# A layer of S4 convolution and gated linear unit: one shuffle for the row exchange, joint table levels, whole casts, and a last stage by channel half

## The chip, the cores and the metric

The kernel runs on one core of a Trainium2 chip. A core has engines that run their own instruction queues side by side and meet through semaphores: TensorE (PE, matrix products, with PEld for its weight loads), VectorE (DVE), ScalarE (ACT), GpSimd (POOL) and SyncE (SP), which issues most DMAs. Operands lie in SBUF (128 partitions); PE writes to PSUM, from where DVE or ACT copy ("evacuate") to SBUF. The metric is the device time of one execution in microseconds, the median of several runs.

## The reference

With x = A_u of shape (1, 2048, 512) and layernorm xn of x over the 512 channels, the output is x + A(xn) + B(xn).

```python
def _A_ref(u, A_re, A_im, B_re, B_im, C_re, C_im, log_dt, Dskip):
    dt = jnp.exp(log_dt)[:, None]
    logdA, dB = dt * A, dt * Bc            # A, Bc, Cc complex, (512, 128)
    P = jnp.exp(logdA[:, :, None] * l[None, None, :])     # l = 0..2047
    K = jnp.einsum("dn,dnl,dn->dl", Cc, P, dB).real
    ...                                     # y = causal convolution of u with K along the tokens (by FFT)
    return y + u * Dskip[None, None, :]

def _B_ref(x, w_gate, w_up, w_down):        # 512 -> 1792 -> 512
    h = _sigmoid(x @ w_gate) * (x @ w_up)
    return h @ w_down
```

So branch A is a long convolution of each channel with a kernel made of 128 complex modes, and branch B is a gated linear unit.

## The kernel before

The program is a list of about 940 operations (`pl.add`, `pl.copy`), each with its engine, its dependences and the buffer slots that it takes and frees. A table written out by hand, `ORDER` (L207 on), gives the order in which `run` (L293 on) emits them, and so the order of every engine's queue. `ON_DVE` (L205) names by operation number the copies that go to DVE (L288) rather than ACT (L290); `UEV` (L204) names the up products that ACT evacuates (L1066), so that DVE multiplies them from SBUF (L1070).

In order of time, but heavily interleaved:

1. Warm-up products (L526), loads, and the layernorm of 16 tiles of 128 tokens: statistics L547 and L548, normalizing on ACT (L555) or DVE (L560). Tokens 0 to 511 are transposed by PE and evacuated by ACT (L576); the other three groups of four tiles go through DRAM (`x_scr`) and a transposing DMA.
2. Parameters of the modes (L613 and around), then a ladder of twelve powers (k = 0 to 11) of each mode's step: square on ACT (L672), the next power on DVE (L679, L681), and a cast of each power to bf16 into the tables `W` (L664 on DVE, L666 on ACT), two instructions a power, one for each channel half.
3. The first stage of the token transform (L698), stored to `z_scr` in DRAM.
4. The kernel tables, by four channel quarters (c = 0 to 3): from a seed copy, levels of complex products double a table `G` (1, 2, 4, 8 columns a level) and others a table `H`. Each product is four DVE instructions: multiplies L737 and L738, then sums L742 and L743, half as wide. Products of the tables on PE (L821), evacuation (L290), selection (L841) give the kernel's transform `kT`.
5. For each channel half (p = 0, 1; 256 channels) eight units: load from `z_scr`, product with the constant `m2` (L892), evacuation to `xx`, exchange of neighbouring groups of 32 partitions into the second row of `xx` (p = 0: four DMAs of 64 KB from SBUF to SBUF; p = 1: four DVE copies, L905), load of the constant `E` (320 KB), product with `kT` (L914), evacuation, elementwise products on DVE (L919, L923), product with the constant `mab` (L936), evacuation, and a store to `v_scr` in DRAM. The constants `m2` and `mab` are loaded once and serve both halves.
6. The gated unit, by four groups of 512 tokens: gate (L1031), up (L1055), sigmoid (L1043), product (L1070), down (L1099), fourteen products a tile. GpSimd's DMA adds x into the result (`glu_sb` for the first two groups).
7. The last stage, `final` (L999 on), for t = 0 to 5, two token tiles each: four products 512 wide (L995), one DVE sum (L1010) of the result and the down product's tile into a buffer of the pool `ot`, and an output DMA of 256 KB with runs of 2 KB. The last group of tokens is added by L1119.

The pools have few slots: two pairs of PSUM banks (pool `s`) are shared by stages 3 to 5 and 7, four single banks (pool `gu`) belong to the gated unit, three buffers each hold `xx` and `E`. PE runs its queue strictly in order, so that a product that waits holds up all that follow.

Of the kernel before, what the change touches and what calls it, by code (L numbers as in the profile page):

```python
# [12 lines left out]
I32 = mybir.dt.int32  # L13
# [7 lines left out]
D = 512  # L21
# [15 lines left out]
NU = 16  # L37
# [143 lines left out]
def _consts():  # L181
# [17 lines left out]
    for q in range(8):  # L199
        sr[q, q // 2, 31 + 32 * ((q ^ (q // 2)) % 2)] = 1.0  # L200
    return dict(SR=f(sr), ident=f(np.eye(128)), S1=f(np.tile(S1, (4, 1))), S2=f(np.stack([_build_S2(by), np.roll(_build_S2(by), 32, axis=1)], axis=1)), M2=f(quads(M2[by])), SW=f(sw),
                MAB=f(np.stack([quads(MA[by], True), quads(MB[by], True)], axis=2)), E=f(_build_E(M2, by).reshape(128, NU // 2, 2, NKT, 128).transpose(1, 0, 2, 3, 4)))

UEV = (3, 5, 8, 9, 10, 11, 15, 16, 17, 18, 19, 20, 21, 23, 24, 26, 27, 28, 29, 30, 31, 32, 33, 34, 35, 36, 37, 38, 39, 40, 41, 42, 43, 44, 45, 54)  # L204
ON_DVE = (64, 67, 73, 76, 97, 98, 110, 121, 122, 123, 124, 482, 836, 838)  # L205
ON_ACT = (2,)
ORDER = [  # L207
    1, 24, 0, 23, 2, 34, 25, 27, 4, 3, 6, 26, 33, 35, 37, 28, 36, 29, 30, 38, 43, 44, 46, 39, 40, 45, 10, 7, 13, 19,
    20, 31, 32, 21, 41, 48, 42, 22, 592, 604, 593, 605, 615, 618, 624, 47, 90, 88, 91, 49, 11, 103, 5, 14, 104, 89,
    606, 50, 102, 92, 93, 12, 627, 653, 658, 9, 633, 54, 594, 654, 55, 634, 610, 655, 101, 656, 106, 598, 611, 659,  # L210
    635, 599, 105, 616, 617, 619, 51, 94, 636, 56, 600, 95, 96, 97, 107, 657, 52, 628, 620, 621, 637, 15, 114, 622,
    643, 644, 57, 178, 108, 8, 98, 115, 645, 58, 625, 623, 110, 116, 53, 59, 640, 648, 142, 641, 601, 602, 626, 646,
    595, 596, 649, 143, 60, 117, 186, 631, 647, 612, 61, 613, 650, 629, 119, 109, 62, 63, 630, 597, 603, 614, 632, 65,
    99, 145, 638, 177, 118, 607, 660, 651, 100, 16, 661, 639, 180, 215, 168, 608, 652, 64, 66, 187, 609, 662, 642, 67,
    68, 169, 147, 704, 150, 726, 699, 148, 727, 179, 181, 190, 170, 151, 663, 149, 69, 127, 70, 188, 120, 664, 71, 121,
    171, 700, 665, 671, 72, 73, 172, 74, 189, 111, 130, 131, 146, 666, 75, 76, 122, 128, 216, 191, 77, 124, 192, 711,
    672, 705, 194, 195, 123, 125, 157, 158, 78, 159, 673, 709, 193, 719, 712, 79, 80, 196, 710, 160, 720, 739, 217,
    721, 740, 722, 724, 674, 679, 152, 197, 81, 82, 725, 680, 198, 173, 83, 723, 199, 713, 729, 684, 730, 686, 734,
    736, 737, 183, 112, 113, 685, 126, 84, 687, 200, 174, 86, 728, 201, 688, 735, 153, 154, 202, 689, 746, 690, 744,
    747, 745, 731, 667, 161, 738, 748, 203, 175, 85, 732, 204, 733, 129, 696, 184, 155, 205, 176, 716, 694, 697, 695,  # L220
    691, 692, 132, 714, 87, 715, 698, 206, 218, 207, 219, 717, 182, 706, 681, 775, 701, 693, 718, 135, 18, 185, 133,
    208, 210, 702, 707, 211, 682, 683, 136, 703, 220, 741, 144, 225, 233, 708, 742, 134, 156, 227, 209, 817, 812, 234,
    235, 162, 743, 237, 221, 813, 805, 230, 165, 238, 236, 749, 224, 806, 163, 241, 222, 242, 228, 226, 243, 223, 137,
    164, 17, 166, 244, 138, 139, 140, 141, 375, 239, 232, 229, 262, 675, 167, 750, 751, 752, 245, 246, 212, 757, 759,
    231, 758, 818, 213, 249, 810, 247, 240, 248, 250, 263, 251, 252, 214, 253, 811, 450, 376, 451, 377, 760, 452, 264,
    815, 800, 254, 255, 257, 265, 816, 814, 776, 275, 795, 272, 796, 258, 435, 378, 379, 381, 359, 777, 457, 274, 256,
    266, 819, 797, 765, 267, 280, 268, 281, 282, 309, 269, 283, 284, 259, 798, 801, 260, 261, 285, 454, 436, 820, 270,
    825, 273, 821, 360, 455, 382, 380, 456, 288, 277, 766, 453, 778, 826, 780, 781, 289, 799, 458, 459, 767, 785, 290,
    779, 442, 768, 437, 782, 383, 783, 278, 460, 291, 827, 802, 384, 438, 465, 367, 441, 439, 271, 461, 462, 361, 292,
    786, 769, 784, 286, 385, 293, 362, 828, 829, 463, 822, 790, 443, 823, 444, 276, 287, 386, 803, 279, 420, 440, 294,  # L230
    824, 310, 792, 851, 852, 466, 472, 390, 365, 445, 311, 364, 464, 296, 793, 467, 387, 412, 388, 791, 787, 832, 446,
    295, 298, 297, 794, 312, 299, 368, 830, 807, 369, 313, 788, 391, 392, 789, 447, 808, 448, 770, 473, 804, 300, 809,
    301, 363, 471, 366, 468, 405, 772, 370, 314, 474, 831, 771, 773, 302, 304, 319, 303, 305, 853, 856, 427, 394, 371,
    327, 833, 469, 470, 475, 397, 393, 395, 389, 449, 406, 421, 328, 774, 476, 407, 320, 329, 321, 422, 834, 331, 913,
    863, 398, 413, 914, 323, 854, 315, 332, 835, 396, 408, 330, 322, 496, 564, 426, 335, 399, 414, 316, 372, 477, 336,
    324, 837, 855, 337, 373, 374, 317, 338, 400, 326, 478, 857, 339, 340, 401, 318, 306, 428, 307, 429, 341, 308, 520,
    492, 342, 325, 343, 411, 425, 479, 568, 843, 493, 402, 345, 864, 403, 753, 761, 494, 333, 346, 344, 334, 423, 347,
    348, 424, 410, 430, 540, 845, 431, 349, 351, 838, 350, 352, 432, 565, 836, 433, 901, 404, 409, 906, 902, 415, 416,
    495, 353, 516, 528, 552, 566, 541, 354, 844, 881, 355, 569, 908, 567, 542, 882, 417, 570, 907, 434, 517, 903, 418,
    909, 518, 543, 556, 921, 419, 521, 497, 522, 571, 572, 861, 573, 498, 519, 523, 529, 846, 574, 910, 530, 883, 886,  # L240
    904, 524, 480, 504, 544, 905, 499, 508, 553, 862, 575, 525, 884, 554, 526, 885, 555, 865, 858, 557, 558, 545, 500,
    859, 839, 546, 866, 527, 484, 358, 847, 501, 502, 559, 560, 481, 911, 482, 561, 485, 868, 912, 562, 887, 589, 586,
    563, 547, 486, 915, 548, 483, 487, 505, 503, 532, 580, 356, 916, 509, 917, 506, 871, 510, 549, 869, 550, 551, 488,
    489, 872, 490, 491, 357, 891, 888, 583, 533, 896, 867, 873, 892, 507, 511, 531, 512, 893, 587, 874, 534, 513, 535,
    536, 537, 897, 514, 889, 894, 515, 898, 895, 875, 576, 918, 890, 870, 876, 899, 919, 878, 538, 539, 590, 588, 582,
    581, 577, 860, 578, 877, 591, 585, 579, 920, 900, 879, 880, 922, 840, 848, 925, 841, 842, 584, 849, 923, 926, 676,
    668, 850, 677, 669, 678, 670, 924, 927, 929, 762, 763, 930, 933, 754, 928, 764, 755, 756, 935, 934, 936, 931, 932,
    937, 939, 940, 938]
# [72 lines left out]
def kernel(  # L321
# [21 lines left out]
    pl = _Plan(dict(s=NS, gu=NGU, hT=NHT, zs=4, zx=2, xx=3, es=3, kb=2, pp=2, pq=2, vs=2, ot=3, tg=2, us=2, sq=2))  # L343
# [53 lines left out]
    for nm, sz in [("W1", 12 * KB), ("gc", 2 * KB), ("G", 16 * KB), ("H", 20992), ("tmp", 4 * KB), ("W0", 12 * KB),  # L397
                   ("xn", 16 * KB), ("lad", 16 * KB), ("kx", 8 * KB), ("zs", 4 * KB), ("pq", 2 * KB)]:
        OFF[nm] = o
        o += sz  # L400
# [5 lines left out]
    W = [at(OFF["W%d" % p], [12, 2, DW]) for p in range(NP)]  # L406
# [67 lines left out]
    l_m2 = load("SP", m2[:], cten["M2"].ap(), 256 * KB, pkt=2048)  # L474
# [186 lines left out]
    def f_cast(cur, k, dve):  # L661
        for p in range(NP):
            if dve:
                V.tensor_copy(out=W[p][:, k], in_=cur[:, :, DW * p:DW * p + DW])  # L664
            else:
                S.activation(out=W[p][:, k], in_=cur[:, :, DW * p:DW * p + DW], func=ACT.Identity)  # L666
# [59 lines left out]
    def cmul(lo, outp, n, m, conj, buf, deps, prio):  # L726

        ne = n * NPR * 4
        wide = lambda v: v.rearrange("p r c k h -> p r c (k h)")
        mre = m[:, 0, :].rearrange("p (r h) -> p r h", h=2).unsqueeze(2).to_broadcast([128, NPR, 2 * n, 2])  # L730
        mim = m[:, 1, :].rearrange("p (r h) -> p r h", h=2).unsqueeze(2).to_broadcast([128, NPR, 2 * n, 2])
        sl = _Slot(buf)
        tb = lambda: at(TMP[buf][sl.idx], [2048])[:, 0:ne].rearrange(
            "p (r c k h) -> p r c k h", r=NPR, c=2, h=2)
# [14 lines left out]
    for c in range(4):  # L749
# [5 lines left out]
        gdep = kgen.get(c - 2, [])  # L755
        hdep = kgen.get(c - 1, [])

        last = pl.copy(nc, 0.32, G[:, :, :, 0, :].rearrange("p r c h -> p c r h"),
                       gc[:, :, cs].rearrange("p c (r h) -> p c r h", h=2), [o_g] + gdep, PC)
        n = 1  # L760
        for lev in range(4):
            st = min(n, 8)
            for q in range(0, n, st):
                last = cmul(G[:, :, :, q:q + st, :], G[:, :, :, n + q:n + q + st, :], st, W[c // 2][:, 4 + lev, :, ws],
                            True, "tg", [last, W_op[4 + lev]], PC)
            n *= 2
# [428 lines left out]
```

## Time and profile before

| | us |
|---|---|
| median of three runs (222.06 to 223.08) | 222.13 |
| span of the profiled execution | 219.8 |
| PE, PEld busy | 209.2, 105.0 |
| DVE busy | 202.2 |
| ACT busy | 175.9 |
| POOL busy | 22.6 |
| evacuations and copies on ACT, L290 from 128x1024 PSUM, 63 of 1044 ns | 64.6 |
| sigmoids, L1043, 52 of 643 ns | 32.1 |
| products, L1070, from SBUF 36 of 421 ns; with a PSUM operand 20 of 684 ns | 14.9; 13.2 |
| exchange copies, L905, 32 of 421 ns, from 160.5 to 191.1 | 13.5 |
| DMA traffic | 41.36 MB, 188 GB/s mean |

The profile is one execution. Its span runs from the first to the last recorded instruction; the time of a run holds in addition what lies around it, here 2.3 us. A group's mean is the time of one instruction with what overlaps its neighbours. TensorE's granted clock is 1.00 in nearly every window. The slowest parts are not one after the other: PE, DVE and ACT are all busy most of the time, so what matters is which of them the others wait for in each stretch.

### The profile page before, as it was taken

What the parts mean: (1) busy time and instruction counts of PE and PEld (TensorE: products, weight loads), DVE (VectorE), ACT (ScalarE), POOL (GpSimd) and SP (SyncE); (2) the same over time, 40 slices, a digit from 0 to 9 for tenths busy, and PEclk for the clock granted to TensorE, in tenths of its full rate; (3) what the DMA queues carried; (4) which work ended last, traced back from release to release, by engine and by line L of the source; (5) the groups of instructions that cost most, each with busy time, mean ns of one, the idle gap of its engine ahead of it and who ended that gap; (6) DMA issues with size and microseconds to landing.
All of it is one profiled execution on the core that took longest, in us unless ns stands there. A gap on an engine that the chain in (4) does not pass through costs nothing.

```text
span 219.8 us, 5357 instructions
## 1 busy us (share of the span) xinstructions
PE 209.2 (95%) x2075; PEld 105.0 (48%) x2103; DVE 202.2 (92%) x444; ACT 175.9 (80%) x283; POOL 22.6 (10%) x39
## 2 busy tenths in 40 slices
PE   7999988999999999999999999999989999999994
PEld 2544433444434454445555555554555455543453
DVE  3999999999999999999999999999989999993582
ACT  3699999999999999769899999977578978942000
POOL 2216001001000049100000004000020100000000
PEclk9999999999999999999999999999999999999999
DMA  5997069216667064526818579856857987688743
GB/s 172 333 425 298 7 180 317 80 42 143 237 134 206 18 198 97 202 82 178 244 55 237 152 244 210 212 173 169 228 111 236 265 265 232 189 234 209 220 158 136
DMA packets 40651, 41.36 MB, mean 188 GB/s; under 512 B 9009, under 2 KB 31922, under 8 KB 40498
## 3 DMA queue, kind: packets, MB, share of 16 engines
q1 hardware_dynamic: 39458, 39.12, 57.7%
q0 software_dynamic: 864, 1.57, 4.9%
q10 hardware_dynamic: 304, 0.33, 0.6%
q8 instruction: 16, 0.26, 0.5%
q14 instruction: 9, 0.07, 0.1%
HBM read 25.28 MB, written 12.06 MB: 170 GB/s over the span
## 4 chain that ended last, share of the span: by engine, by line
DVE 48%; PE 41%; DMA 4%; ACT 4%; issue 2%; POOL 0%; DVEq 0%; ACTq 0%
PE bank L1099 11%; DVE big L738 7%; PE pair L914 7%; DVE big L737 6%; PE bank L1031 6%; PE bank L1055 6%; DVE hT_sb L1070 6%; PE pair L936 5%; DVE stats L547 4%; DVE big L742 4%; DVE big L743 3%; DVE big L679 3%; DVE big L681 3%; DMA big<-c_E 3%; ACT big L290 3%; DVE big L613 2%
## 5 line engine op out<-in xcount | busy, mean ns | idle before, releaser
L290 ACT ACTIVATE big<-pair 128x1024 bf16<-128x1024 f32 (+2 forms) x75 | 73.4, 996 | 9.2 <-PE pair L936 1.9
L1055 PE MATMUL bank<-xnT,wu_sb 128*128 128x512 bf16 x214 | 54.4, 379 | 2.5 <-ACT us_sb L1066 1.3
L1031 PE MATMUL bank<-xnT,wg_sb 128*128 128x512 bf16 (+1 forms) x211 | 50.9, 367 | 1.4 <-ACT xnT L576 0.4
L1099 PE MATMUL bank<-wd_sb,hT_sb 128*128 128x512 bf16 (+1 forms) x230 | 50.2, 366 | 0.4
L1043 ACT ACTIVATE hT_sb<-bank 128x512 bf16<-128x512 f32 x52 | 32.1, 643 | 3.8 <-PE bank L1031 3.6
L1031 PEld LDWEIGHTS <-wg_sb 128*128 128x128 bf16 x236 | 21.9, 98 | 26.4 <-issue 5.2
L1099 PEld LDWEIGHTS <-hT_sb 128*128 128x128 bf16 x238 | 22.5, 98 | 24.8 <-issue 2.1
L1055 PEld LDWEIGHTS <-wu_sb 128*128 128x128 bf16 x224 | 21.0, 97 | 27.2 <-issue 5.4
L737 DVE TENSOR_TENSOR big<-big 128x1024 bf16<-128x1024 bf16 (+4 forms) x40 | 26.8, 670 | 0.1
L738 DVE TENSOR_TENSOR big<-big 128x1024 bf16<-128x1024 bf16 (+4 forms) x40 | 26.6, 666 | 0.0
L1066 ACT ACTIVATE us_sb<-bank 128x512 bf16<-128x512 f32 x36 | 22.4, 634 | 0.0
L919 DVE TENSOR_TENSOR big<-big 128x2048 bf16<-128x2048 bf16 x16 | 19.5, 1219 | 0.4
L914 PE MATMUL pair<-big 128*128 128x256 bf16 x160 | 19.8, 272 | 0.1
L914 PEld LDWEIGHTS <-big 128*128 128x128 bf16 x160 | 15.5, 98 | 4.9 <-issue 1.1
L790 ACT ACTIVATE sq_sb<-big 128x256 bf16<-128x256 bf16 (+2 forms) x20 | 13.7, 685 | 3.9 <-DVE big L743 3.8
L743 DVE TENSOR_TENSOR big<-big 128x512 bf16<-128x512 bf16 (+4 forms) x40 | 16.6, 414 | 0.0
L742 DVE TENSOR_TENSOR big<-big 128x512 bf16<-128x512 bf16 (+4 forms) x40 | 16.5, 413 | 0.0
L290 ACT ACTIVATE big<-big 128x256 bf16<-128x256 bf16 x36 | 15.7, 470 | 0.2
L1070 DVE TENSOR_TENSOR hT_sb<-hT_sb,us_sb 128x512 bf16<-128x512 bf16 x36 | 14.9, 421 | 0.0
L905 DVE COPY big<-big 32x1024 bf16<-32x1024 bf16 x32 | 13.5, 421 | 0.5
L1070 DVE TENSOR_TENSOR hT_sb<-hT_sb,bank 128x512 bf16<-128x512 bf16 x20 | 13.2, 684 | 0.5 <-PE bank L1055 0.5
L936 PE MATMUL pair<-big 64*64 64x512 bf16 (+1 forms) x256 | 12.8, 326 | 0.5 <-ACT big L290 0.2
(103 smaller groups left out, 222.2 us busy)
## 6 DMA issues: line engine op xcount, KB each, us to landing
big<-c_E SPq DMA_DIRECT2D x16, 320.0 KB, 4.4
z_scr<-big SPq DMA_DIRECT2D x16, 256.0 KB, 3.0
big<-z_scr SPq DMA_DIRECT2D x16, 256.0 KB, 3.5
v_scr<-big SPq DMA_DIRECT2D x16, 256.0 KB, 2.9
big<-in_A_u_dram SPq DMA_DIRECT2D x4, 512.0 KB, 8.5
big<-big SPq DMA_DIRECT2D x32, 64.0 KB, 3.1
big<-v_scr SPq DMA_DIRECT2D x4, 512.0 KB, 5.0
wu_sb<-in_B_w_up_dram SPq DMA_DIRECT2D x2, 896.0 KB
```

What stands on the lines that cost most here:

```text
L290: nc.scalar.activation(out=get(out), in_=get(in_), func=ACT.Identity)
L737: V.tensor_tensor(out=wide(outp), in0=wide(lo), in1=mre, op=ALU.mult)
L738: V.tensor_tensor(out=wide(tb()), in0=wide(lo), in1=mim, op=ALU.mult)
L742: V.tensor_tensor(out=outp[:, :, 0], in0=outp[:, :, 0], in1=tb()[:, :, 1], op=opr)
L743: V.tensor_tensor(out=outp[:, :, 1], in0=outp[:, :, 1], in1=tb()[:, :, 0], op=opi)
L914: T.matmul(two(sk)[:, o:o + DW], es()[:, g, kt, :], kT[p][:, kt, :], start=kt in (0, NKT - 1), stop=kt >= NKT - 2)
L936: T.matmul(two(sv)[o:o + 64, DW * (2 * g + y):2 * DW * (g + 1)], mab[b:b + 64, 2 * u + g, q, :], pq()[b:b + 64, q, ch] if y else pp()[b:b ...
L1031: T.matmul(bank(sl, k % 2)[:, c0:c1], w_at(w, CUT_G, kt, k), xnT[:, grp, kt, c0:c1], start=(kt == 0), stop=(kt == KT - 1))
L1043: S.activation(out=hT_sb[:, hs.idx, k % 2, :], in_=bank(sl), func=ACT.Sigmoid)
L1055: T.matmul(bank(sl), w_at(wu_sb, CUT_U, kt, k), xnT[:, grp, kt, :], start=(kt == 0), stop=(kt == KT - 1))
L1070: V.tensor_tensor(out=h(), in0=h(), in1=us_sb[:, us.idx, :] if on else bank(sl), op=ALU.mult)
L1099: T.matmul(bank(po)[:, 0:c[1] - c[0]], hT_sb[:, hts[k // 2].idx, k % 2, jj * 128:(jj + 1) * 128], wd_sb[:, k, c[0]:c[1]], start=first and ...
```

## The change

The same result is computed. Six things differ.

- **Exchange of the second half (p = 1).** The four copies a unit become one `stream_shuffle` of 128 partitions by 512 int32 elements, which swaps neighbouring partitions within each group of 32. The rows of the constants are laid out to match, so `M2`, `MAB` and `E` now exist once for each half; `m2` (256 KB) is loaded again after the last L892 of the first half, `mab` (512 KB) after the last L936 of the first half.
- **Joint low levels.** For an even quarter c the seed and the levels of 1, 2 and 4 columns are made for quarters c and c+1 in one go (256 channels); the level of 8 stays with its quarter.
- **Whole casts.** A power is cast by one instruction of 1024 columns for both channel halves; `W0` and `W1` lie side by side for it.
- **Last stage.** `final` goes by group of four token tiles and channel half: eight products 256 wide, one DVE sum straight into the result's buffer, one output DMA of 256 KB with runs of 512 bytes. The first channel half's finals need only the first half's loads.
- **Engines.** 24 rather than 14 copies and normalizings are named in `ON_DVE` (with all normalizing from tile 4 on), 39 rather than 36 in `UEV`. Casts of the powers 0, 3 and 8 are on DVE, before those of 3, 4, 6 and 7.
- **Order.** `ORDER` is another list throughout. At the start, all warm-up products come ahead of the transposes; the first gate products are of full width, before four were of half the width.

```diff
+    pair = np.arange(32).reshape(2, 16)
+    alt = np.concatenate([(32 * np.array([[0], [1]]) + 2 * (pair % 16) + c).reshape(32) for c in range(2)])
+    alt = np.concatenate([alt, 64 + alt])
...
+    m2b[..., alt[0:64]], mabb[alt], eb[..., alt] = m2, mab, e
+    return dict(..., M2=f(np.stack([m2, m2b])), SW=f(sw),
+                MAB=f(np.stack([mab, mabb])), E=f(np.stack([e, eb])))
...
     def f_cast(cur, k, dve):
-        for p in range(NP):
-            if dve:
-                V.tensor_copy(out=W[p][:, k], in_=cur[:, :, DW * p:DW * p + DW])
-            else:
-                S.activation(out=W[p][:, k], in_=cur[:, :, DW * p:DW * p + DW], func=ACT.Identity)
+        src = cur.rearrange("p c (w d) -> p w c d", w=NP)
+        if dve:
+            V.tensor_copy(out=W_all[:, :, k], in_=src)
+        else:
+            S.activation(out=W_all[:, :, k], in_=src, func=ACT.Identity)
...
-        for lev in range(4):
-            st = min(n, 8)
-            for q in range(0, n, st):
-                last = cmul(G[:, :, :, q:q + st, :], G[:, :, :, n + q:n + q + st, :], st, W[c // 2][:, 4 + lev, :, ws],
-                            True, "tg", [last, W_op[4 + lev]], PC)
-            n *= 2
+        if c % 2 == 0:
+            G2 = at(OFF["G"], [2 * NPR, 2, NGE, 2])
+            last = pl.copy(nc, 0.48, G2[:, :, :, 0, :].rearrange("p r c h -> p c r h"),
+                           gc[:, :, DW * (c // 2):DW * (c // 2) + DW].rearrange("p c (r h) -> p c r h", h=2),
+                           [o_g] + kgen.get(c - 2, []) + hdep, PC)
+            for lev in range(3):
+                n = 1 << lev
+                last = cmul(G2[:, :, :, 0:n, :], G2[:, :, :, n:2 * n, :], n, W[c // 2][:, 4 + lev], True, "tg",
+                            [last, W_op[4 + lev]], PC)
+            g_part = last
+        g_done = cmul(G[:, :, :, 0:8, :], G[:, :, :, 8:16, :], 8, W[c // 2][:, 7, :, ws], True, "tg", [g_part, W_op[7]], PC)
...
+        if p:
+            l_m2 = dma("SP", m2[:], cten["M2"].ap()[1], deps=fm_op, prio=45, pkt=2048)(256 * KB)
+            l_mab = dma("SP", mab, cten["MAB"].ap()[1], deps=fv_op, prio=46, pkt=4096)(512 * KB)
...
                 def f_sw(xx=xx):
-                    for b in range(4):
-                        V.tensor_copy(out=half_of(xx, b, 1), in_=half_of(xx, b ^ 1, 0))
+                    q = lambda j: xx()[:, j].rearrange("p h m -> p (h m)").bitcast(I32)
+                    V.stream_shuffle(out=q(1), in_=q(0), mask=[i ^ 1 for i in range(32)])
...
-    def final(t, gdeps):
-        sl, osl = _Slot("s"), _Slot("ot")
+    def final(g, p, gdeps):
+        sl, cs = _Slot("s"), slice(DW * p, DW * p + DW)
+        res = (glu_sb[:, 4 * g:4 * g + 4, :] if g < 2 else at(TAIL["glu"], [4, D]))[:, :, cs]
...
-            for r in range(2):
-                s2_mm(t, r, bank(sl, r), True, (0, D))
+            for q in range(4):
+                for j in range(2):
+                    T.matmul(two(sl)[64 * j:64 * j + 64, DW * q:DW * q + DW], s2[:, q % 2, :], vall[:, g, p, j, q, :], start=True,
+                             stop=True, tile_position=(0, 64 * j), skip_group_check=True)
...
-            V.tensor_tensor(out=ot().rearrange("p r d -> p (r d)"), in0=two(sl), in1=res.rearrange("p r d -> p (r d)"), op=ALU.add)
+            V.tensor_tensor(out=res, in0=two(sl).rearrange("p (q d) -> p q d", q=4), in1=res, op=ALU.add)
...
-        dma("SP", outv[:, isl, :], lambda: ot(), deps=[fin], prio=1, rel=[osl], pkt=2048)(256 * KB)
+        dma("SP", outv[:, 4 * g:4 * g + 4, cs], lambda: res, deps=[fin], prio=1, pkt=512)(256 * KB)
```

## The prediction

> **What bounds the kernel now.** I read first the engines' totals, then the windows along the span, then the chain of waits, then the groups of instructions and the DMA issues.
>
> ```profile
> PE 209.2 (95%) x2075; PEld 105.0 (48%) x2103; DVE 202.2 (92%) x444; ACT 175.9 (80%) x283; POOL 22.6 (10%) x39
> ```
> ```profile
> core 0: us, PE busy (x) PEld busy (x) DVE busy (x) ACT busy (x) POOL busy (x), PEclk, DMA share, GB/s
> ...
> 30.00:50.00 20.00, 18.71 (x96) 8.02 (x98) 19.93 (x51) 19.80 (x35) 1.26 (x2) 1.00 0.47 145
> 50.00:70.00 20.00, 19.66 (x101) 8.46 (x102) 20.00 (x46) 20.00 (x35) 1.07 (x1) 1.00 0.67 176
> ...
> 130.00:150.00 20.00, 19.67 (x315) 11.22 (x319) 20.00 (x40) 17.47 (x29) 2.22 (x4) 1.00 0.78 206
> ...
> 160.00:180.00 20.00, 19.11 (x233) 10.94 (x234) 18.81 (x35) 17.37 (x22) 1.54 (x3) 1.00 0.81 218
> 180.00:200.00 20.00, 19.70 (x177) 10.30 (x180) 18.48 (x36) 13.59 (x19) 0.00 (x0) 1.00 0.78 224
> 200.00:219.80 19.80, 16.35 (x106) 8.43 (x104) 9.69 (x11) 0.59 (x1) 0.00 (x0) 0.99 0.57 176
> ```
> PE is busy 209.2 of 219.8 us, so 10.6 us are all that any order could win. Of these 1.4 lie ahead of the first matmul and 3.5 behind the last (add, store, landing). Some 5.7 us lie inside. From 30 to 150 us DVE is full, and PE is not: PE waits there for a full DVE. From 160 us both have gaps. The chain says the same:
>
> ```profile
> 84.63 1.13 DVE big L737
> 85.76 1.14 DVE big L738
> 87.54 1.09 DVE big L737
> ```
> ```profile
> 155.94 1.42 PE L821 MATMUL pair<-big 128*32 128x82 bf16 x128
> ...
> 161.63 0.44 PE L841 MATMUL pair<-big,sw 128*32 128x96 bf16 x24 [0.62 <-issue]
> ```
> The first fence has pieces of the chain (start, time on the chain), the second PE's timeline at the fourth quarter's tables (start, time, work, idle before). The chain runs from start to start of DVE's instructions, so it shows the price of one in a full queue, the step: an L737 of 1024 columns has a mean of 686 ns in the groups but a step of 0.60. I use steps where instructions follow each other, since each overlaps the next by some 0.08 us.
>
> ```profile
> L905 DVE COPY big<-big 32x1024 bf16<-32x1024 bf16 x32 | 13.5, 421 | 0.5
> L737 DVE TENSOR_TENSOR big<-big 128x1024 bf16<-128x1024 bf16 x16 | 11.0, 686 | 0.0
> L681 DVE TENSOR_TENSOR big<-big 128x512 f32<-128x512 f32 x11 | 7.6, 691 | 0.0
> L1010 DVE TENSOR_TENSOR big<-pair,glu_sb 128x1024 bf16<-128x1024 f32 x4 | 4.7, 1220 | 3.2 <-PE pair L995 3.2
> L664 DVE CAST big<-big 128x512 bf16<-128x512 f32 x8 | 3.1, 427 | 0.0
> ```
> ```profile
> big<-c_E SPq DMA_DIRECT2D x16, 320.0 KB, 4.4
> ...
> v_scr<-big SPq DMA_DIRECT2D x16, 256.0 KB, 2.9
> ...
> big<-c_MAB SPq DMA_DIRECT2D x1, 512.0 KB, 4.4
> ```
>
> **How far PE is behind.** I added the steps of PE's groups in its own order and compared with its real starts. PE is 0.6 us late at the first full gate matmul (12.7 us), 3.5 at the first down product (41.5), 4.8 at L821 of the fourth quarter (155.94 against 151.2 of work), 5.5 behind the L841 wait, 6.65 at the last down product (213.3). Most of the loss is therefore made by 156 us, where DVE's results are the gate.
>
> **The change on DVE.** Exchange: 32 copies of 0.42 (13.5 us) become 8 shuffles. No row shows a shuffle. Below it lies the 0.42 of a copy with the same columns on a quarter of the partitions; above it the 1.68 of the four copies that it replaces. I take 0.60, the step of L681, the nearest in columns and width (512 of 4 bytes): 4.8 us, so -8.7.
>
> The Trainium skill ("VectorE: DVE Perf Modes", section "The perf-mode tier table") speaks against it: a copy of bf16 in SBUF has a 4x mode, STREAM_SHUFFLE only the 1x mode, some 2400 ns for 2048 elements. Its formula for 1x, (N+151)/0.96, gives an estimate of 691 ns for 512 elements, which the trace's L681 agrees with; charged by 1024 bf16 elements it would be 1224, and the exchange would win 3.7 rather than 8.7.
>
> Joint levels: for each pair of quarters, 24 instructions of levels 1, 2, 4 become 12 of twice the width. By the groups' means level 1 goes from 2x1288 ns to 1461, level 2 from 2x1461 to 2220, level 4 from 2x2220 to 3838: -2.4 a pair, less 12 overlaps of 0.08: -1.4, and -2.8 for two pairs. Casts: 8 of 0.34 (step) become 3 of 0.60, -0.9. Normalizing: five tiles move here from ScalarE (L555 to L560), +5x0.33 = +1.6. Copies that move here: three PSUM evacuations of 1024 (L288, 1.20), two of 512 or less (0.6), and small ones: +5.3. Three more up products are evacuated by ScalarE, so their L1070 reads SBUF (0.34 rather than 0.60): -0.8. Sum -6.3 us. The last-stage adds stay six of 1.2.
>
> ScalarE: -3.5 (five L555 of 0.70), -2.75 (three of 0.915), some -1.9 (small copies), +0.3 (nine wide casts of about 0.95 for sixteen of 0.52), +1.5 (three L1066 of 0.49): -6.4. PE's columns stay the same; four s2 matmuls of 512 become eight of 256.
>
> **What of that reaches the end.** Only what a gate releases earlier. At L821 of the four quarters I set PE's summed work ahead of the gate against the DVE work that it needs. Before: 73.2 against 74.1, 95.5/96.2, 126.4/127.1, 151.2/151.8: DVE is 0.6 to 0.9 more. In the new order: 77.4/76.7, 95.2/94.4, 130.4/128.8, 152.0/150.9: DVE is 0.7 to 1.6 less. At the fourth, before, DVE's 151.8 us of work were done at 155.9, so it had lost 4.1. I give it 0.4 more in the new order, since it comes to normalize tiles 8 to 11 before their load. Then 150.9 + 4.5 = 155.4, against 152.0 of PE work: PE is 3.4 late instead of 4.8; the second quarter gives 3.4 to 3.5 likewise. **-1.3 us.** Most of the 6.3 us can't be seen: ahead of the fourth gate DVE's work falls by 0.9 only, since the moved copies and tiles take back what levels and casts give, and the exchanges come mostly behind it, where PE has 8.5 us more work ahead of its last L936 than DVE.
>
> The 0.8 at L841 has no releaser that the trace names; half a chance to stay, so -0.4, bounds -0.8 to 0. From 162 to 213 us PE falls another 1.1 behind, with L936 of five units at 0.4 to 0.8 us of margin to DVE; the new order has 5 or more: -0.5, bounds -1.1 to 0. Start: all warm matmuls are first and the gate matmuls wait for both halves of the transposed tokens. PE may be 0.2 to 0.4 later at 12 us, but 3.4 us come later from DVE anyway, so the cover costs nothing; without it, +0.4.
>
> **Reloads.** The second half needs another m2 and mab. m2 (256 KB, 3 us by the v_scr store) has some 11 us of PE work between its last reader and its first new one. mab waits for the last first-half L936; it landed 4.4 us after issue, and 6.6 us of PE work lie until the next L936. Behind that wait stand in SP's queue a v_scr store, two E loads and the first v load. I take +0.2, bounds 0 and +1.0 (it lands with the E loads' contention).
>
> **End.** Output pieces keep 256 KB but have runs of 512 bytes; the v_scr store with such runs lands in 2.9, the 2-KB runs in 2.5. One is near the end, in a shared queue: +0.2, bounds 0 and +0.5.
>
> Sum: -1.3 -0.4 -0.5 +0.2 +0.2 = -1.8, span 219.8 to 218.0. The median of 222.13 stands 2.3 above the profiled span, with start and end outside; I keep this: **220.3 us**.
>
> **Rivals.** (1) No change (221.0 to 223.2). The lateness is not DVE's: ScalarE is full from 20 to 80 us too (19.80 and 20.00 of 20), so its queue might make the same 1.3. Against it: its work falls by 6.4, mostly before 100 us. Or startup loses what the gates win. The sum without the three gains is 222.13 + 0.4 = 222.5.
> (2) Slower: the last unit's way through DRAM. Its L936 comes at 192.4 us of PE work, before at 188.3. Behind it are the evacuation 0.92, the store 2.9 and a load (issue 0.5, landing 2.4 at least), 6.7 to 7.0, while PE has 7.4 to 7.6 us of work before it needs the rows. It decides from 7.5 us on: store and load at 5.0 each (the median of the 512-KB v loads) give 0.9 + 5.0 + 0.5 + 5.0 = 11.4, a stall of 3.9, and 224.2. For it: v_scr stores and now output pieces of 512-byte runs share the end, with a DMA share of 0.78 already from 180 us. Against it: the v_scr stores had 2.9 at that share.
> (3) Slower: the shuffle is slow. With PE 3.4 late and DVE 4.5, the smallest margin of second-half L936 is 7.2 - 1.1 = 6.1 behind seven shuffles, so 0.87 each: it decides above 1.47 us. At 1.68 it costs 1.5 (221.8), at 2.4 it costs 6.5 (226.8). The exchange then does not do what it says.
> (4) Larger gain: the tables' gates stop binding, because DVE loses nothing at the start and ScalarE's relief also ends the 0.9-us waits of L1055 for L1066 (2.5 us of lateness by 30). PE ends 2.5 to 3 late rather than 6.65: 218.3.
>
> **Chances.** Forecast 0.45, (1) 0.25, (2) 0.13, (3) 0.07, (4) 0.10. A measurement tells 0.5% (1.1 us) from no change: faster 0.55, same 0.25, slower 0.20. The likeliest case's own range is 219.0 to 221.0. Over all, 217.8 (all bounds at their good end: -1.3 -0.8 -1.1, and 1.1 of the start's waits) to 223.6, which leaves out most of (2) and (3).
>
> **What would show it.** Right: one shuffle of 0.6 to 0.7 us a unit; DVE's total near 196, ScalarE's near 169.5; PE 3.4 us late at the fourth quarter's L821, and after 160 us DVE idle for PE in most units. Wrong: PE waiting for mab or for the v rows in the last 30 us; DVE still full and PE late by 4.8 at L821; a shuffle above 1.5; or a PE gap at 12 to 16 us, where weights come in a new order, of more than the 3.4 us that follow.

## The result, and the profile after

The changed kernel takes 228.66 us (median of four runs, 227.94 to 232.24); the kernel before, on the same chip, 222.6. The ratio is 1.027, interval 1.023 to 1.031: slower by some 6 us, where 220.3 was forecast. The 232.24, and the 234.78 among the runs of e13_copies_back below, were run in a slower state, and the ratios leave such runs out. The profiled execution spans 226.8 us against 219.8.

The engines' totals of the changed kernel, and what PE waited for longest:

```profile
PE 210.8 (93%) x2127; PEld 106.9 (47%) x2127; DVE 201.7 (89%) x410; ACT 170.0 (75%) x266; POOL 17.2 (8%) x39
```
```profile
PE pair L826 <- DVE big L747: 1.8, 3, 1.0
PE bank L1006 <- DMA big<-v_scr: 1.6, 1, 1.6
...
PE bank L1067 <- issue: 1.3, 1, 1.3
...
PE pair L846 <- issue: 1.0, 1, 1.0
```
ScalarE came to 170.0 (forecast 169.5), VectorE to 201.7 (forecast 196): its total hardly fell. In these lines PE waits three times for VectorE at the tables (L826, which was L821), once for rows of `v_scr`, and twice for nothing that the profile names. The fourth quarter's tables, which began at 155.94 us before, now begin here:

```profile
161.95 1.67 PE L826 MATMUL pair<-big 128*32 128x82 bf16 x128 [0.29 <-DVE big L747]
```
The windows that answer to those of before (columns as in the prediction):

```profile
30.00:50.00 20.00, 19.59 (x110) 8.26 (x108) 19.76 (x47) 19.81 (x31) 2.61 (x6) 1.00 0.67 210
130.00:150.00 20.00, 18.45 (x308) 10.00 (x310) 19.67 (x43) 17.68 (x30) 2.12 (x4) 1.00 0.64 160
160.00:180.00 20.00, 18.49 (x325) 11.20 (x323) 16.98 (x34) 14.01 (x20) 2.26 (x3) 1.00 0.86 230
```
The start is better than before (30 to 50 us: PE 19.59 against 18.71), the middle worse (130 to 150: 18.45 against 19.67), and from 160 us on VectorE idles as forecast. The groups of the new instructions:

```profile
L742 DVE TENSOR_TENSOR big<-big 128x1024 bf16<-128x1024 bf16 x14 | 9.7, 692 | 0.3
L916 DVE STREAM_SHUFFLE big<-big 128x512 int32<-128x512 int32 x8 | 5.7, 724 | 0.0
L668 DVE CAST big<-big 128x1024 bf16<-128x1024 f32 x3 | 2.0, 671 | 0.0
```
The shuffle has a mean of 724 ns, and a step of 0.62 to 0.64 where the next instruction follows at once: near the 0.60 taken. Each instruction costs what was forecast, and the durations of all VectorE's instructions, summed, fall from 234.4 to 228.6 us, by 5.8. What grew lies between them. VectorE's timeline before, where an instruction follows one that it does not read (start, time, work):

```profile
85.64 1.26 DVE L738 TENSOR_TENSOR big<-big 128x2048 bf16<-128x2048 bf16 x1
86.77 0.39 DVE L795 TENSOR_TENSOR big<-sq_sb 128x384 bf16<-128x384 bf16 x1
```
And in the changed kernel, where multiplies and sums of one table product follow each other (L742 and L743 are now the multiplies, L747 and L748 the sums):

```profile
80.78 0.27 DVE L801 TENSOR_TENSOR big<-big 128x128 bf16<-128x128 bf16 x1
81.09 0.69 DVE L742 TENSOR_TENSOR big<-big 128x1024 bf16<-128x1024 bf16 x1
81.69 0.68 DVE L743 TENSOR_TENSOR big<-big 128x1024 bf16<-128x1024 bf16 x1
82.41 0.42 DVE L747 TENSOR_TENSOR big<-big 128x512 bf16<-128x512 bf16 x1
```
L738 ends at 86.90, and L795 starts at 86.77, before that end. L743 starts 0.09 before the end of L742, which it does not read. L747 reads what L742 and L743 wrote, and the trace has it wait for a semaphore that L743 raises: L743 ends at 82.37, and L747 starts at 82.41. The same holds from L801 (end 81.05) to L742 (81.09). Over the whole trace the second of two neighbours usually starts 85 ns before the first has ended; where it reads the first, some 35 ns behind it: 0.12 us lost for each such pair. I count a pair as stalled, by time alone, if the start lies between 40 ns before and 160 ns behind the end. Ahead of the fourth quarter's first L821 there are 26 such pairs (together 3.2 us above the usual -85 ns) in the kernel before, and 67 (8.4 us) in the changed one. Of the 67, 21 go from a multiply L743 to a sum L747, and 13 from L748 or L801 to a multiply L742; of the 26, only 3 go into the sums or multiplies of a table product.

This table goes through all runs: the stalled pairs and the time lost in them, and VectorE's longer gaps, all ahead of the fourth quarter's tables; when PE reaches these; and the end of PE's last matmul. All but the medians are from one profiled execution.

| kernel | median us (ratio to before, interval) | pairs, us | longer gaps | fourth tables | last matmul |
|---|---|---|---|---|---|
| before | 222.1 to 222.6 | 26, 3.2 | 0.4 | 155.9 | 216.5 |
| changed | 228.66 (1.027, 1.023 to 1.031) | 67, 8.4 | 1.0 | 162.0 | 223.6 |
| e1_spread | 236.49 (1.065, 1.057 to 1.073) | 38, 4.7 | 9.2 | 169.0 | 231.7 |
| e2_close | 229.20 (1.030, 1.027 to 1.033) | 69, 8.3 | 1.9 | 162.5 | 223.9 |
| e3_down_early | 227.81 (1.025, 1.022 to 1.027) | 66, 8.4 | 1.4 | 162.5 | 222.2 |
| e4_shuffle_only | 222.88 (1.003, 1.001 to 1.005) | 30, 3.8 | 0.8 | 156.4 | 218.3 |
| e5_dve_queue | 228.88 (1.028, 1.025 to 1.031) | 46, 5.8 | 2.2 | 160.8 | 222.5 |
| e6_new_order | 235.10 (1.058, 1.054 to 1.063) | 40, 5.1 | 5.1 | 165.0 | 228.6 |
| e7_before_new_order | 237.43 (1.067, 1.062 to 1.071) | 31, 4.0 | 7.0 | 163.6 | 232.7 |
| e8_no_reload | 229.58 (1.031, 1.026 to 1.037) | 66, 8.4 | 0.9 | 161.8 | 222.7 |
| e9_dve_and_down | 226.99 (1.022, 1.019 to 1.025) | 44, 5.6 | 2.5 | 160.7 | 220.6 |
| e10_near_order | 228.40 (1.026, 1.020 to 1.032) | 40, 5.1 | 2.0 | 160.0 | 223.7 |
| e11_before_near_order | 228.60 (1.029, 1.025 to 1.034) | 28, 3.4 | 2.7 | 158.7 | 222.5 |
| e12_spaced_bursts | 227.11 (1.025, 1.018 to 1.032) | 42, 5.2 | 3.4 | 161.4 | 221.1 |
| e13_copies_back | 233.20 (1.046, 1.041 to 1.052) | 68, 8.6 | 5.0 | 164.8 | 226.3 |

### The profile page after: what moved, and what is told of

The parts are those of the page before. It is cut to its first block, busy times and chain, and to the rows that moved or that the text cites. A ratio compares the mean times of both kernels' runs of the same rounds, so it can differ in the third digit from the quotient of the medians.

```text
span 226.8 us, 5395 instructions
## 1 busy us (share of the span) xinstructions
PE 210.8 (93%) x2127; PEld 106.9 (47%) x2127; DVE 201.7 (89%) x410; ACT 170.0 (75%) x266; POOL 17.2 (8%) x39
## 4 chain that ended last, share of the span: by engine, by line
DVE 43%; PE 28%; ACT 13%; DMA 8%; issue 4%; SPq 1%; POOL 0%; DVEq 0%; ACTq 0%
DVE big L742 7%; DVE big L743 7%; PE pair L925 5%; PE bank L1067 5%; PE bank L1043 5%; DVE hT_sb L1082 5%; DVE big L748 4%; DVE big L747 4%; PE bank L1111 4%; PE pair L947 4%; ACT hT_sb L1055 3%; DMA big<-big 3%; DMA big<-v_scr 2%; ACT big L293 2%; DVE big L617 2%
## 5 line engine op out<-in xcount | busy, mean ns | idle before, releaser
L293 ACT ACTIVATE big<-pair 128x1024 bf16<-128x1024 f32 (+2 forms) x71 | 69.0, 994 | 14.4 <-PE pair L947 4.6
L1067 PE MATMUL bank<-xnT,wu_sb 128*128 128x512 bf16 x224 | 54.5, 379 | 2.5 <-issue 1.3
L1067 PEld LDWEIGHTS <-wu_sb 128*128 128x128 bf16 x224 | 21.1, 98 | 27.5 <-issue 5.8
L1055 ACT ACTIVATE hT_sb<-bank 128x512 bf16<-128x512 f32 x52 | 30.8, 627 | 2.2 <-PE bank L1043 2.2
L742 DVE TENSOR_TENSOR big<-big 128x1024 bf16<-128x1024 bf16 (+4 forms) x34 | 26.0, 764 | 0.7
L1078 ACT ACTIVATE us_sb<-bank 128x512 bf16<-128x512 f32 x39 | 24.3, 633 | 2.5 <-DVE hT_sb L1082 1.3
L743 DVE TENSOR_TENSOR big<-big 128x1024 bf16<-128x1024 bf16 (+4 forms) x34 | 25.8, 757 | 0.0
L795 ACT ACTIVATE sq_sb<-big 128x256 bf16<-128x256 bf16 (+2 forms) x20 | 13.7, 683 | 7.4 <-DVE big L748 5.8
L747 DVE TENSOR_TENSOR big<-big 128x512 bf16<-128x512 bf16 (+4 forms) x34 | 15.8, 464 | 0.7
L1082 DVE TENSOR_TENSOR hT_sb<-hT_sb,us_sb 128x512 bf16<-128x512 bf16 x39 | 15.7, 417 | 0.8 <-ACT hT_sb L1055 0.6
L293 ACT ACTIVATE big<-big 128x256 bf16<-128x256 bf16 (+1 forms) x33 | 14.8, 478 | 1.6 <-PE pair L826 1.2
L748 DVE TENSOR_TENSOR big<-big 128x512 bf16<-128x512 bf16 (+4 forms) x34 | 15.6, 459 | 0.0
L551 DVE BATCH_NORM_STATS2 stats<-big 128x6 f32<-128x512 bf16 x15 | 10.1, 676 | 3.8 <-DMA big<-in_A_u_dram 3.8
L676 ACT ACTIVATE big<-big 128x1024 f32<-128x1024 f32 x11 | 12.1, 1101 | 1.1 <-DVE big L685 1.1
```

The lines of the kernel that those rows point to most:

```text
L293: nc.scalar.activation(out=get(out), in_=get(in_), func=ACT.Identity)
L742: V.tensor_tensor(out=wide(outp), in0=wide(lo), in1=mre, op=ALU.mult)
L743: V.tensor_tensor(out=wide(tb()), in0=wide(lo), in1=mim, op=ALU.mult)
L747: V.tensor_tensor(out=outp[:, :, 0], in0=outp[:, :, 0], in1=tb()[:, :, 1], op=opr)
L748: V.tensor_tensor(out=outp[:, :, 1], in0=outp[:, :, 1], in1=tb()[:, :, 0], op=opi)
L1055: S.activation(out=hT_sb[:, hs.idx, k % 2, :], in_=bank(sl), func=ACT.Sigmoid)
```

## The experiments

Theory A was that dependent neighbours on VectorE make its tables late. Theory B was that the copies moved to VectorE, and the waits for other engines, do it. Theory C came later: PE's stops without a releaser are a lack of instructions. Each run's text says what A and B forecast for it, and in some of them (e4, e6, e10) the letters stand for that run's own two cases. Kernels that differ in `ORDER` alone have the same instructions; their line numbers shift by up to ten, with the longer or shorter table.

**e2_close**, the kernel before with dependent operations put together. Thirty such moves, one of them:

```diff
 ORDER (VectorE's operations only; 169: the multiplies of a level, 170: its sums; 190: multiplies of another table)
-    169, 190, 170,
+    169, 170, 190,
```


> The kernel before with thirty operations of its table products (L742 and L743, the sums) moved up in VectorE's queue to stand right behind the multiplies that they read, nothing else changed; dependent neighbours among the table products go from 3 to 43. Theory A: 40 x 0.12 = 4.8 us more of VectorE time ahead of the tables' gates, where VectorE is full: the time rises from 222.6 by 3.5 to 5 us. Theory B: no change within 0.7 us, as the instructions and their durations are the same.

It takes 229.20, 6.6 us more than before, with the same instructions on every engine. The stalled pairs go from 26 to 69, and the time in them from 3.2 to 8.3: 5.1 us, and 1.5 us of longer gaps besides. The fourth tables come 6.6 us later. The time rose by more than the 3.5 to 5 us of theory A. VectorE is busy 206.3 us, 4.1 more than before, by the same instructions:

```profile
PE 212.7 (94%) x2103; PEld 105.5 (46%) x2103; DVE 206.3 (91%) x444; ACT 176.5 (78%) x283; POOL 16.8 (7%) x39
```
Multiplies and their sums on VectorE's timeline of this kernel:

```profile
85.66 0.44 DVE L745 TENSOR_TENSOR big<-big 128x512 bf16<-128x512 bf16 x1
86.01 0.45 DVE L746 TENSOR_TENSOR big<-big 128x512 bf16<-128x512 bf16 x1
86.49 0.33 DVE L750 TENSOR_TENSOR big<-big 128x256 bf16<-128x256 bf16 x1
```
L746 ends at 86.46, and L750 starts at 86.49. Theory A's price is shown here, where nothing but the order was changed; theory B forecast no change.

**e1_spread**, the other way round, in the changed kernel:

```diff
 ORDER (VectorE's operations only; 203: differences of squares, 206: multiplies that read them, 207: sums; 681, 686: products of the gated unit)
-    203, 206, 207, 681, 686,
+    203, 681, 206, 686, 207,
```


> The changed kernel with its queue on VectorE reordered and nothing else: of the 36 places where an operation of the table products stands right behind the operation whose result it reads, 28 get an independent operation of the same queue between them. Theory A (a VectorE instruction that stands right behind the one it reads from starts 0.12 us later than one behind an independent one, and 41 more such pairs ahead of the fourth quarter's tables cost 5 us): some 28 x 0.12 = 3.4 us of VectorE time go, less what the moved operations cost; the time falls from 228.7 by 2 to 3.5 us, and the stalled pairs ahead of the fourth L826 from 67 to about 40. Theory B (the loss is the copies that VectorE took over and the waits for other engines): within 0.7 us of the changed kernel.

The pairs fell as forecast (67 to 38, 3.7 us less), and the time rose to 236.49. VectorE's waits for ScalarE, among others:

```profile
DVE big L810 <- ACT sq_sb L805: 4.4, 6, 1.0
...
DVE big L301 <- ACT big L303: 3.2, 1, 3.2
```
The operations that were moved up still waited for ScalarE, and VectorE, which keeps its order, waited with them: the longer gaps go from 1.0 to 9.2. The sign is a miss for both theories. The run doesn't tell them apart, since the moves brought waits of their own. TensorE's clock fell as well: the granted clock is 0.50 for 3.4 us at 104.7 and again at 169.5 us, each time behind PE stops (1.5 and 4.7 us the last ones). By estimate, half the clock for 3.4 us costs PE up to 1.7 us each time.

**e5_dve_queue**: as e1, but something is put between two dependent operations only if its inputs were there by then in the changed kernel's trace.

> The changed kernel with VectorE's queue in another order and all other queues as they were. Unlike e1_spread, where operations were moved up that still waited for ScalarE, an operation goes between two dependent ones only where the changed kernel's trace has its inputs ready by then; dependent neighbours on VectorE go from 59 to 33 operations. Theory A (the changed kernel's loss is mostly VectorE's queue order, with the stalls of dependent neighbours in it): the time falls from 228.7 to between 224.5 and 226.5. Theory B (the loss lies in the instructions themselves or in other queues): above 227.5.

Stalled time falls by 2.6 us, longer gaps rise by 1.2, the fourth tables come 1.2 earlier. The time stays the same, a miss for theory A. PE's longest wait shows where most of it went:

```profile
PE bank L1016 <- DMA big<-v_scr: 2.5, 1, 2.5
```
It was 1.6 in the changed kernel. The median also holds runs with a lower clock: the one at a mean granted clock of 0.999 took 227.72, the three at 0.985 to 0.992 took 228.65 to 229.38.

**e3_down_early** and **e9_dve_and_down**. In e3 the third down product of the last group (917) goes ahead of the products that wait for `v_scr`; e9 has this and a reordered VectorE queue from 45 us on.

```diff
-    747, 748, 833, 834, 914, 921, 570, 911, 836, 573, 749, 835, 837, 838, 917,
+    747, 748, 833, 834, 917, 914, 921, 570, 911, 836, 573, 749, 835, 837, 838,
```


> The changed kernel with the third down product of the last group moved ahead of the four small products that wait for the last rows of v_scr, nothing else. The changed kernel's PE waits 1.6 us there. If this wait is on the path that sets the end, the time falls by 1.3 to 1.7 us; if the last transfers to DRAM set the end anyway, by less than 0.5.

> The changed kernel with VectorE's queue reordered from 45 us on (dependent neighbours 59 to 34 operations, the start left as it is) and the third down product ahead of the products that wait for v_scr, as in e3_down_early. In e5_dve_queue the fourth quarter's tables came 1.2 us earlier and the wait for v_scr grew by 0.9 and took most of it back. Theory A (the stalls of dependent neighbours and the wait for v_scr are both on the path): 2 to 4 us below the changed kernel's 228.7, that is 224.7 to 226.7. Theory B (they are not): above 227.5.

e3 takes 227.81, 0.85 less, and its last matmul ends 1.4 earlier; its interval overlaps that of the changed kernel, and 0.85 lies between its two cases. e9 takes 226.99, 1.7 less, between theory A's 226.7 and theory B's 227.5, and its interval (1.019 to 1.025) still meets that of the changed kernel (1.023 to 1.031). That speaks for the stalls and the wait being on the path but doesn't show it for each, and what came back is smaller than what was lost.

**e6_new_order** and **e7_before_new_order**: all queues in another order, with dependent operations apart.

> The changed kernel's instructions, with all queues in a new order that keeps dependent neighbours on VectorE apart (19 instead of 59) and moves the last unit and the down products so that PE does not wait for v_scr. Theory A (order alone loses the 6 us): the time falls to 218 to 222, at or below the kernel before. Theory B (the change's instructions cost more than they save): it stays above 224.

> The instructions of the kernel before, with all queues in an order found in the same way. If what the change saves on VectorE and ScalarE reaches the end, this stays 1 us or more above e6_new_order; if PE's 209.7 us of work bound both once the order is good, the two are within 1 us of each other, and both near 218 to 221.

Both missed by 13 us or more. In both, PE stops early in the start (2.8 us at 8.7 us in e6), and then this (a window of e6_new_order, columns as above):

```profile
10.00:20.00 10.00, 7.05 (x45) 5.13 (x46) 8.38 (x21) 9.19 (x13) 0.17 (x1) 0.66 1.02 423
```
The granted clock falls to 0.66 from 10 to 20 us, where the kernel before and the changed one have 1.00; the first down product comes at 47.2 us instead of 42.2. Behind it PE waits for DMAs whose place in SyncE's queue had moved (2.1 us for `z_scr`, 1.0 for `E` in e6). e6 lies on its theory B's side, and e7 is 2.3 us above e6, as its first case has it, but with these starts, and with two more stretches at a lower clock in e7, the two tell nothing of the theories.

**e10_near_order** and **e11_before_near_order**: nearer orders, with the start and SyncE's queue as they were.

> The changed kernel's instructions from 45 us on in an order in which operations of PE, VectorE and ScalarE are moved by up to twelve places in the list at a time (dependent neighbours 59 to 32), SyncE's queue and the start unchanged. Theory A (the order, not the instructions, loses the time): 220 to 225. Theory B: above 227.

> The kernel before, reordered in the same way from 30 us on. Its dependent neighbours are few already (16 to 20 operations), so theory A leaves little to win: 220.5 to 223, against 222.3 for the kernel before. If the reordering itself and not the apart-standing of dependent operations were what helps e10_near_order, it would fall by as much as that does.

e10 takes 228.40, on theory B's side. It gets the fourth tables to 160.0, and loses that behind them: a stop of 2.0 us without a releaser in the selection (L856, up to 165.17 us), and then half the clock for 3.4 us:

```profile
166.80:170.20 3.40, 3.40 (x17) 1.82 (x14) 3.08 (x6) 1.02 (x1) 0.67 (x1) 0.50 0.87 208
```
Three of its four runs have a mean granted clock of 0.992 and took 227.95 to 229.26; the one at 1.00 took 226.47, 2 us less than the 228.48 of a run of the changed kernel at 1.00, and still outside the 220 to 225 of theory A. The kernel before gets 6 us slower by such a reordering, though it has few dependent neighbours before and after (26 and 28 pairs). That is a miss, and theory A doesn't cover it. Its own order hides waits (2.3 us for `z_scr`, 1.7 for `v_scr`, 1.3 in L849) that the other order shows. No order tried here beats it.

**e4_shuffle_only**, the exchange alone, in the kernel before:

```diff
-                    for b in range(4):
-                        V.tensor_copy(out=half_of(xx, b, 1), in_=half_of(xx, b ^ 1, 0))
+                    q = lambda j: xx()[:, j].rearrange("p h m -> p (h m)").bitcast(I32)
+                    V.stream_shuffle(out=q(1), in_=q(0), mask=[i ^ 1 for i in range(32)])
```


> The kernel before with one shuffle a unit in the place of the four copies L905, nothing else; the constants keep the old layout and are not loaded again, so the second half's rows are multiplied with constants that do not match the exchange: the work is the same, the values are not. Theory A (the exchange lies behind the last gate that VectorE sets): VectorE's total falls by 8 us, the time by 0.3 to 1.3. If the shuffle itself were the loss, the time would rise.

VectorE's total falls to 194.6, by 7.6, and the time does not: 1.003, interval 1.001 to 1.005. The gain is off the path; the 0.3 to 1.3 us hoped for are a miss.

**e8_no_reload**:

```diff
-            l_m2 = dma("SP", m2[:], cten["M2"].ap()[1], deps=fm_op, prio=45, pkt=2048)(256 * KB)
-            l_mab = dma("SP", mab, cten["MAB"].ap()[1], deps=fv_op, prio=46, pkt=4096)(512 * KB)
+            l_m2 = pl.add("SP", 0.0, lambda: None, (), 45)
+            l_mab = pl.add("SP", 0.0, lambda: None, (), 46)
```


> The changed kernel without the second loads of m2 and mab: the second half multiplies with the first half's constants, so its values do not match, and the work is the same otherwise. As predicted, the reloads cost 0 to 0.5 us, so the time stays within 0.7 of 228.7. If the reload of mab were what holds the second half up, it would fall by 1 us or more.

229.58, 0.9 above the changed kernel where less than 0.7 either way was expected, with an interval that overlaps the changed kernel's. It did not get faster: the reloads cost nothing that can be measured.

**e13_copies_back**:

```diff
-ON_DVE = (55, 64, 79, 95, 96, 97, 98, 108, 109, 110, 111, 121, 122, 123, 124, 265, 340, 404, 482, 510, 514, 745, 829, 831,)
+ON_DVE = (55, 64, 79, 97, 98, 110, 121, 122, 123, 124, 265, 340, 482, 745, 829, 831)
```


> The changed kernel with the three evacuations of 1024 columns and the five normalizings that the change put on VectorE given back to ScalarE, the order as it is. Theory B (taking them over is what made VectorE late): VectorE's total falls by 5, the fourth quarter's tables come 1.5 us or more earlier, and the time falls by 1.5 to 3 us. Theory A: only the five normalizings (1.6 us) and one evacuation stand ahead of the gates, and ScalarE takes them in its fullest stretch, so the time changes by less than 1.2 us either way.

VectorE's total falls to 197.1, ScalarE's rises to 176.5, and the time rises by 4.5. VectorE's two longest waits for ScalarE:

```profile
DVE hT_sb L1082 <- ACT us_sb L1078: 4.0, 3, 1.8
...
DVE big L291 <- ACT hT_sb L1055: 2.0, 1, 2.0
```
Now it waits for ScalarE. Theory B's sign is refuted: taking these copies over did help, in this order. Theory A's "less than 1.2 us either way" is a miss too.

**e12_spaced_bursts**, for PE's stops. PE's timeline in e9, of which it is an edit:

```profile
137.16 1.42 PE L836 MATMUL pair<-big 128*32 128x82 bf16 x128
138.52 0.39 PE L1077 MATMUL bank<-xnT,wu_sb 128*128 128x512 bf16 x1
141.02 0.59 PE L1077 MATMUL bank<-xnT,wu_sb 128*128 128x512 bf16 x2 [2.11 <-issue]
```
```diff
 ORDER (PE's operations only; 295, 297: the two halves of L836, 846, 841: up products)
-    295, 297, 846, 399, 851, 841,
+    295, 846, 841, 297, 399, 851,
```


> e9_dve_and_down with two up products (eight wide matmuls) moved between the two halves of L836 of the third quarter's tables, nothing else. In e9 PE stops for 2.1 us in the middle of an up product at 139 us with nothing to wait for; a fetch of 16 KB on the queue of kind instruction began at 137.8, and PE had issued 175 matmuls and weight loads in the 3 us before. Theory C (PE runs out of instructions behind a burst of small matmuls, and goes on when the fetch has landed, some 2.5 to 3 us after its start): with the burst spread the stop shrinks below 0.8 us and the time falls by 1 to 2 us, to 225 to 226. Rival (a hidden wait for a buffer of the up product): the stop stays at 1.5 us or more, wherever the halves stand.

```profile
137.27 0.80 PE L836 MATMUL pair<-big 128*32 128x82 bf16 x64
138.25 1.89 PE L1077 MATMUL bank<-xnT,wu_sb 128*128 128x512 bf16 x8 [0.18 <-ACT hT_sb L1065]
140.06 0.75 PE L836 MATMUL pair<-big 128*32 128x82 bf16 x58
141.22 0.25 PE L836 MATMUL pair<-big 128*32 128x82 bf16 x6 [0.41 <-issue]
```
The up products no longer stop; what is left is 0.41 us in the second burst, and it ends 2.3 us after this run's fetch began (138.87). The stop follows theory C and not its rival. The forecast of the time, 225 to 226, is a miss: it stays at 227.11, since at the fourth tables PE now waits 0.85 for VectorE, which sets that point.

## Why the prediction was wrong, and where it was right

**The step that failed** is in the gates: "Then 150.9 + 4.5 = 155.4, against 152.0 of PE work: PE is 3.4 late instead of 4.8". PE was 10.0 late, since its fourth tables came at 162.0. The work, 150.9, was right to about 1 us. The 4.5 of lost time was not, and came to 11.1 (162.0 - 150.9): it took the 4.1 that the kernel before loses as a property of the kernel, when it belongs to its order. The sum was made of steps measured where neighbours are independent, as they mostly are before. The new order has 41 more stalled pairs ahead of that gate, at 0.12 each. The account of the 6.0 us from 155.9 to 162.0: -0.9 of work (as forecast), +5.2 in stalled pairs (8.4 - 3.2), +0.6 of longer gaps, and 1.1 that I do not assign. That such pairs cost what they seem to is shown by e2; that they are these 5.2 us of the changed kernel is the trace's count. The runs that took some of them away (e5, e9, e10) got 1.2 to 2.0 of 2.6 to 3.4 us back at the gate, while the longer gaps grew, and no run that took pairs out of the changed kernel came below 226.99. So the cost is shown by experiment in the kernel before, and only in part in the changed one.

Nor does all of it reach PE as a wait for VectorE. PE's waits ahead of the fourth tables grow from 4.1 to 9.6 us: 2.9 more for VectorE, 1.5 more for ScalarE, 1.1 more without a releaser. In e2, where only VectorE's order was changed, they grow by the same 2.9 and 1.5, and by 0.6 for a DMA, so VectorE's lateness can reach PE through ScalarE too. The 1.1 without a releaser are mostly a stop of 1.3 us at 140.7 us, told of in the last section. After it PE had only 0.3 us to wait for VectorE at the fourth tables: by then PE was nearly as late as VectorE.

The prediction's premise was also too strong for the kernel before. It reads there that "PE waits there for a full DVE", but ahead of 156 us PE's waits name ScalarE for 2.1 us and VectorE for 0.4, and the line at 155.94 shows no wait: the gate that was to win 1.3 us did not hold PE up at that point.

The Trainium skill ("VectorE: DVE Perf Modes", section "The DRAIN you can't avoid") says that the next instruction does not start until the pipe of the one ahead is empty, that one which is not held starts earlier, and that a semaphore after each of eight copies cost nothing extra. The trace has the early start, 85 ns before the profiled end; but a follower that reads the one ahead starts some 35 ns behind that end, and 43 more such pairs made e2 slower by 3.0%.

**Behind the gate** the kernel lost another 1.1 us. Rival (2) came true in part: PE waited 1.6 us for `v_scr`. The stores landed in 2.7 us (median) against the 2.9 taken; the last loads of 128 KB took 6.4 and 6.7 rather than the 2.4 that I took as the least, so this term was mis-sized:

```profile
big<-v_scr SPq DMA_DIRECT2D x2, 128.0 KB, 6.7
big<-v_scr ACTq DMA_DIRECT2D x2, 128.0 KB, 6.4
```
L846's stop is 1.0 instead of L841's 0.6, so the 0.4 booked there did not come. By the prediction's sums PE has 0.8 less work there.

**Right:** the shuffle's price; ScalarE's total; that the exchange's gain lies off the path (e4: 7.6 us less work, no gain), though a gain of 0.5 from 162 us on was still booked and did not come; that the start's delay is mostly hidden (PE is 1.3 late at 12 us against 0.6 before by the prediction's sums; its idle time up to the first down product is 4.4 us against 4.0); that the reloads cost next to nothing; that VectorE idles for PE behind 160 us. **VectorE's total** of 196 was wrong by 5.7, mostly for the reason above: the summed durations fell by 5.8, about the 6.3 forecast, but without the overlap of neighbours they cover more of the span.

Rivals (1), (3) and (4) fell. **Open:** why the joint levels ended in an order with so many dependent neighbours. One chain of four levels for two quarters has fewer independent partners than two chains; this is argued, and a per-quarter form in the new order was not tried. Nor is it shown that an order exists in which the changed instructions beat the kernel before.

## What to carry to other kernels

Before summing an engine's instructions for a new order, mark which of them read the result of the one just ahead, and price those pairs apart: here 0.12 us each, 5.2 us ahead of the fourth tables, where the change saved 0.9 of work by forecast. An order fitted to one set of instructions is a part of the kernel's speed; carry the lost time of a queue over to another order only after counting its dependent neighbours, its engine waits and its bursts anew. Work saved on an engine behind the last point at which it gates others was worth nothing here (e4).

## What the runs showed of the hardware

PE can run out of instructions. The DMA queues of the changed kernel hold this line (packets, MB, share):

```profile
q8 instruction: 16, 0.26, 0.5%
```
Its packets are of 16 KB, and one is fetched for about every 256 matmuls and weight loads of PE. Two halves of L826 are 256 of these in 1.5 us. In the DMA records, fetches start at 139.08 and 165.78 us of the changed kernel, and the stops in the middle of L1067 and L846 end at 141.97 and 168.21: 2.9 and 2.4 us later. In the kernel before one starts at 159.17, and the stop in L841 ends at 161.63, 2.5 later. It is so in every trace: in the fifteen of this case PE has 21 stops of 0.25 us or more without a releaser, and each ends 1.2 to 1.6 us after the end of such a packet, 2.3 to 3.2 us after its start. Most of the 16 fetches of a run bring no stop. The Trainium skill ("Runtime: NRT & Kernel Launch", section "Instruction fetch mechanics") gives blocks of 16 KB, or 256 instructions, which agrees, and takes their fetch as mostly hidden; behind bursts of small matmuls it was not, with stops of up to 2.5 us (e7, at 167.0 us).

The other surprise is the clock. In five stretches of 3.4 us and two of 6.8 us, all in e1, e6, e7 and e10, the granted clock is 0.50, and each stretch begins in a PE stop or at most 1.7 us behind one: 2.8 us in e6 and 1.4 and 1.0 in e7 at the start (hence the 0.66 of the window from 10 to 20 us), 1.3 and 1.5 and then 4.7 in e1, 2.0 in e10, 2.5 and 2.9 in e7. Other stops left it at 1.00: 0.7 and 1.2 at the start of the changed kernel, 2.1 at 139 us in e9, 2.5 before 212.8 us in e5. So the length of the stop alone doesn't tell, and where the border lies these runs don't show. An order that makes PE stop can lose in this way part of what it won on VectorE.
